# Three moves in a one-core kernel: sums of x over three periods, w_out2 decoded tile by tile earlier, one block's y copied by ScalarE

## The chip, the cores and the metric

The kernel runs on one core of a Trainium2 chip. The metric is the device time of one execution in microseconds (us). Before the change the median of three runs is 885.55 us (884.87 to 888.54).

## What is computed

Attention with a decaying state gives 3072 tokens of 512 values; two feed-forward layers follow. All in float32:

```python
for t in range(S):                      # 4 batches, 8 heads, S = 768, head size 64
    state = gamma * state + einsum('bhd,bhe->bhde', k[:, :, t], v[:, :, t])
    y[:, :, t] = scale * einsum('bhd,bhde->bhe', q[:, :, t], state)
x = y.transpose(0, 2, 1, 3).reshape(3072, 512)
h = x @ w_in                            # 512 x 2048
x = (h - tanh(h)) @ w_out               # 2048 x 512
h = x @ w_in2                           # 512 x 1024
sm = softmax(h)
solu = h * sm
ln = (solu - mean(solu)) / sqrt(var(solu) + 1e-6) * g_ln
out = ln @ w_out2                       # 1024 x 512
...
```

## The kernel before, in words

Each float32 operand of a product is split into a high and a low part (names ending in h and l), and a product is three matmuls: high by high, high by low, low by high. The weights come as 64-bit words and are decoded to float32 on the chip: a load "raw" on SP's queue (L124), an absolute value on ACT (L130), four integer and clamping operations on DVE (L137, L138, L141, L144), for w_out2 a scaling by g_ln on ACT (L152), the high part on ACT (L153) and the low part on DVE (L154). A Decoder object does one of these stages for one tile at a time with `to(stage, upto)`; its `step()` advances the whole line by one tile.

The tokens are worked in six blocks of 512. In order of time:

- 0 to 150 us: attention of the first blocks and the first layer's h of blocks 0 and 1.
- 150 to 238: the first pass, the product with w_out of blocks 0 and 1 (16 steps; the sums and parts of x for the next pair of blocks are made beside it, L580 to L583 and `put_x`). At its end `keep_y` copies four PSUM banks per block to SBUF, even ones by ACT (L388), odd ones by DVE (L386).
- 238 to 428: the second pass, h of blocks 2 to 5, two blocks at a time by a Strassen-like scheme of seven products P1 to P7 on halves of x and w_in, in 16 periods: eight for the pair (2, 3), eight for the pair (4, 5). It needs four sums of halves of x (`x_sums`) and a split of seven operands (`put_x`: high part xh on ACT, low part xl on DVE, L161). What remains of the attention runs between. A product's bank is added to a kept one by DVE (hs, L754) or subtracted from its tanh (L746, on POOL or DVE); only then does its bank come free for a product of a later period.
- 428 to 616: the product with w_out of blocks 2 to 5 (s = 2 to 5 in the code), 16 steps of 2.72 us each; operands g are loaded five steps ahead and split (gp) two steps ahead. The tiles of w_in2 and w_out2 are decoded here, and in the last block the first of six pairs of token groups goes through the second layer.
- 616 to 886: the second layer for the other pairs: product with w_in2 (L883), softmax and layer norm (L898 to L922), transposes (L933, with copies uh on ACT and ul on DVE, L936), product with w_out2 (L947).

In the first pass PE, ACT and part of POOL follow an order fixed in the program; from L700 on PE's order is the order of the code. For all other engines and for SP's queue a scheduler sets the order at build time, from its own estimate of times. Each engine then runs its list strictly in that order.

Of the kernel before, what the change touches and what calls it, by code (L numbers as in the profile page):

```python
# [26 lines left out]
F32 = mybir.dt.float32  # L27
F32R = mybir.dt.float32r
# [8 lines left out]
P = 128  # L37
# [53 lines left out]
def body(ctx: ExitStack, tc, z, w_in, w_out, w_in2, w_out2, g_ln, cst, tab, out):  # L91
# [2 lines left out]
    cpool = ctx.enter_context(tc.tile_pool(name="cpool", bufs=1))  # L94
    big = ctx.enter_context(tc.tile_pool(name="big", bufs=N4))
    mid = ctx.enter_context(tc.tile_pool(name="mid", bufs=N2))
    stp = ctx.enter_context(tc.tile_pool(name="stp", bufs=B + 2))
    yd = ctx.enter_context(tc.tile_pool(name="yd", bufs=1, space=DRAM))

    def pin(ins, on=True):  # L100
# [45 lines left out]
        ), fixed)  # L146

    def stage3(wf, scale, eng, fixed):
        w = t4([P, 2, 512], F32R, "w")
        hi, lo = w[:, 0, :], w[:, 1, :]  # L150
        if scale is not None:
            nc.scalar.activation(wf, wf, AF.Copy, scale=scale)  # L152
        pin(nc.scalar.copy(hi, wf), fixed)  # L153
        pin(eng.tensor_tensor(lo, wf, hi.bitcast(F32), ALU.subtract), fixed)  # L154
        return hi, lo
# [35 lines left out]
            self.to(2, i + 2)  # L191
            self.to(3, i + 1)

    A = ExitStack()
    G = ExitStack()
    xfp = A.enter_context(tc.tile_pool(name="xfp", bufs=1))
    ps_r = G.enter_context(tc.tile_pool(name="ps_r", bufs=4, space=PSUM))
# [181 lines left out]
                    py[e], a[:, cols], x, start=f == 0 and n == 0, stop=f == NF1 - 1 and n == 2  # L379
                )  # L380

    def keep_y(s, py):
        for e in range(NK):
            ysb = t2([P, SB], F32, "ysb")
            if e % 2:
                nc.vector.tensor_copy(ysb, py[e])  # L386
            else:
                nc.scalar.copy(ysb, py[e])  # L388
            nc.sync.dma_start(
                out=y1d[s][:, :, e, :], in_=ysb.rearrange("p (j t) -> p j t", j=B)  # L390
            )
# [66 lines left out]

    com = Combined()
    yl, ys, ysum = {}, {}, {}  # L460

    def load_y(j):
        t = t4([P, 2, NK, P], F32, "yl")
# [105 lines left out]
        wl[n] = views(t[:2], t[2:])  # L569

    def put_x(p, m, eng):
        xs[m] = [t4([P, 2, SB], F32R, f"x{n}") for n in "hl"]
        parts(*xs[m], sums[p][m], eng)

    def x_sums(p, other):

        x0, x1 = xf_of[2 * p], xf_of[2 * p + 1]
        b11, b21, b12, b22 = (x[:, h, :, :] for x in (x0, x1) for h in range(2))
        t1, t2_, t4_ = (t4([P, 2, SB], F32, "xt") for _ in range(3))
        nc.vector.tensor_tensor(t1, b12, b11, ALU.subtract)  # L580
        other.tensor_tensor(b12, b22, b12, ALU.subtract)
        nc.vector.tensor_tensor(t2_, b22, t1, ALU.subtract)
        other.tensor_tensor(t4_, b21, t2_, ALU.subtract)  # L583
        return {P1: b11, P2: b21, P3: b22, P5: t1, P6: t2_, P7: b12, P4: t4_}


    spare = dict(pool=ps_y, tag="y")
# [83 lines left out]
    for n in range(NF1 + 1):  # L671
        if n < NF1:
            while dec1.at[3] < NF1 + n + 1:
                dec1.step()
            if n:
                split_g(n)
            dec1.step()
        if n:
            for b, g in enumerate(gs.pop(n - 1)):
                products_y(n - 1, g, dec1.w[NF1 + n - 1], py2[b])  # L680
        if n in (9, 12, 15):
            load_wq()
        if n in (11, 14):
            combine_w(len(wl))
        if n in (13, 16):
            store_w()
        if n == 4:
            sums[1] = x_sums(1, nc.gpsimd)
        if 8 <= n < 15:
            put_x(1, n - 8, nc.vector)  # L690
        if n == 12:
            load_units(4 * B + 2)
        if n == 15:
            prepare(4 * B, H // 2, True, False)
    for b in range(2):
        keep_y(b, py2[b])
    G.close()


# [20 lines left out]
        else:  # L720
            unit(k, None, True, opool=ps_a)

    def product(left, m, ph, first=True):
        n = 0
        for i in range(2):
            (ah, al), (xh, xl) = ([t[:, i, :] for t in side[m]] for side in (left, xs))
            for a, x in ((ah, xh), (ah, xl), (al, xh)):
                nc.tensor.matmul(  # L728
                    ph, a, x, start=first and n == 0, stop=n == 5, skip_group_check=True
                )  # L730
                n += 1
# [54 lines left out]

    def begin(n):
        b1[n] = bank()
        product(wl[n], P1, b1[n])
        p1[n] = keep(b1[n])  # L790

    def after(n, m):
        if q[n] == (1, NJ1 - 1):
            put_x(2, m, nc.vector)

    begin(0)
    for n in range(len(q) + 1):
# [22 lines left out]
                split_wo(i)  # L820
        if now:
            b3 = bank()
            product(wl[n], P2, b3)
            finish(2 * p, j, summed(b3, p1.pop(n)), nc.gpsimd)
            piece(-1)
            after(n, P2)
            b2[n] = bank()
            product(wl[n], P5, b2[n])
            p5[n] = keep(b2[n])
            store_w()  # L830
            piece(0)
            after(n, P5)
            if todo:
                visit(todo.pop(0))
        if was:
            pp, jj = q[n - 1]
            product(wl[n - 1], P4, b1[n - 1], False)
            finish(2 * pp, jj + NJ1, b1.pop(n - 1), nc.vector)
            after(n - 1, P4)
        if now:  # L840
            product(wl[n], P6, b1[n], False)
            u2[n] = keep(b1[n])
            piece(1)
            after(n, P6)
            if todo:
                visit(todo.pop(0))
        if was:
            product(wl.pop(n - 1), P3, b2[n - 1], False)
            finish(2 * pp + 1, jj, summed(b2.pop(n - 1), u2.pop(n - 1)), nc.gpsimd)
            after(n - 1, P3)  # L850
        if now:
            if n + 1 < len(q):
                piece(2)
                begin(n + 1)
                after(n + 1, P1)
            product(wl[n], P7, b1[n], False)
            piece(3)
            finish(2 * p + 1, j + NJ1, summed(b1[n], p5.pop(n)), nc.gpsimd)
            after(n, P7)
            if todo:  # L860
                visit(todo.pop(0))
        if (p, j) == (1, 5):
            sums[2] = x_sums(2, nc.gpsimd)
    G.close()
    A.close()


    bp = ctx.enter_context(tc.tile_pool(name="bp", bufs=1))
    sp = ctx.enter_context(tc.tile_pool(name="sp", bufs=3))
    ident = bp.tile([P, P], F32, name="ident")  # L870
# [129 lines left out]
    for n, (s, f) in enumerate(steps):  # L1000
# [10 lines left out]
            keep_y(s, py)  # L1011
        if s >= NSB - 3 and n % 2 == 0 and com.n[2] < 12:
            com.step()
        if s == NSB - 1:
            if f % 2 and f > 4:
                dec2.step()
            if f == 0:
                load_y(0)
            if f == 2:
                sum_y(0)  # L1020
                load_y(1)
            if f == 5:
                split_y(0)
            if f == 9:
                sum_y(1)
                load_y(2)
            if f == 8:
                pair = Pair(0)
            for m in {8: (P1, P2), 9: (P6,), 10: (P5,), 11: (P7,), 12: (P4,), 13: (P3,)}.get(f, ()):
                pair.part(m)  # L1030
            if f == 12:
                split_y(1)
            if f == 14:
                sum_y(2)
# [10 lines left out]
    with tc.manual_schedule(engines={mybir.EngineType.PE}):  # L1045
        for j in range(1, NJ + 1):
# [8 lines left out]

            parts2(P1, P2)
            trans(a)
            dec2.step()
            parts2(P6, P5)
            trans(b)  # L1060
            dec2.step()
            if j + 2 < NJ:
                sum_y(j + 2)
            if j + 3 < NJ:
# [61 lines left out]
```

## Time and profile before

| | |
|---|---|
| time, median of 3 runs | 885.55 us (884.87 to 888.54) |
| profiled execution | 888.24 us, span 886.5 us |
| mean granted clock of TensorE in the span | 0.988 |
| PE busy | 842.8 us (95%), 6488 matmuls |
| DVE, ACT, POOL busy | 554.9, 437.3, 272.4 us (63%, 49%, 31%) |
| largest PE waits (table of waits) | 8.8 us for POOL vq (attention), 6.4 for DVE hs, 4.0 for DVE ul, 3.1 for ACT part, 2.9 for DVE gp, 2.4 for DVE ysb |

The profile is of one execution. Engines: PE is TensorE's matmuls, PEld its weight loads, DVE VectorE, ACT ScalarE, POOL GpSimd, SP the engine that issues most transfers. A row of a timeline gives the start and length in us, the engine, the line of the program, the operation, output <- inputs by the program's names, shapes and count; in brackets stands the time for which the engine was idle before it, and what ended that. Consecutive equal operations are drawn together (x4).

### The profile page before, as it was taken

The numbers are of one execution on the slowest core, as the hardware profiler recorded it, in microseconds if no ns is written. First come the engines' busy times: TensorE is split into PE (matmuls) and PEld (weight loads), VectorE is DVE, ScalarE is ACT, GpSimd is POOL, SyncE is SP. The second block draws the span as 40 slices with busy tenths as digits, with TensorE's granted clock in tenths as the row PEclk, the third lists the DMA queues.
The fourth block names the chain that finished last, engine by engine and source line by source line (L and its number), as shares of the span: only waits on it lengthen the run. The fifth ranks groups of instructions, "written<-read, shape, count | busy, mean of one in ns | idle before, by whom it ended". The sixth has DMA issues, their size and how long they took to land.

```text
span 886.5 us, 16612 instructions
## 1 busy us (share of the span) xinstructions
PE 842.8 (95%) x6488; PEld 693.1 (78%) x6488; DVE 554.9 (63%) x1025; ACT 437.3 (49%) x866; POOL 272.4 (31%) x244
## 2 busy tenths in 40 slices
PE   4799999999899988999999999989799999999997
PEld 4678888788777767888788888877688888888886
DVE  3798976999668686234546971397755555555541
ACT  4656644556445555445543451255555555555442
POOL 4410200212234354443201521045444444444200
PEclk8899999999999999999999999999999999999999
DMA  9667862535899518935857370743111111110001
GB/s 363 248 219 258 274 218 72 190 130 198 306 359 317 191 73 310 391 120 178 294 205 244 113 237 24 239 141 98 50 46 47 47 47 48 48 49 24 24 24 48
DMA packets 66462, 144.34 MB, mean 163 GB/s; under 512 B 6608, under 2 KB 19024, under 8 KB 66384
## 3 DMA queue, kind: packets, MB, share of 16 engines
q1 hardware_dynamic: 58032, 128.28, 41.2%
q10 hardware_dynamic: 8352, 15.00, 4.5%
q8 instruction: 51, 0.84, 0.4%
q14 instruction: 27, 0.22, 0.1%
HBM read 94.50 MB, written 48.76 MB: 162 GB/s over the span
## 4 chain that ended last, share of the span: by engine, by line
PE 77%; DVE 11%; DMA 5%; issue 3%; ACT 2%; SPq 1%; POOL 0%; ACTq 0%; POOLq 0%; DVEq 0%
PE py L378 20%; PE ph L728 15%; PE po L947 15%; PE ph L883 12%; PE ph L353 8%; PE out L229 2%; PE ptr L933 2%; PE sc L229 2%; DMA z<-z 2%; DVE wf L141 1%; DVE wcl L161 1%; DMA raw<-w_in 1%; DVE w L154 1%; DVE wf L138 1%; DMA wod<-wf 1%
## 5 line engine op out<-in xcount | busy, mean ns | idle before, releaser
L378 PE MATMUL py<-gp,w 128*128 128x512 f32 x768 | 176.0, 390 | 2.9 <-DVE gp L161 2.9
L378 PEld LDWEIGHTS py<-gp,w 128*128 128x128 f32 x768 | 143.9, 188 | 34.0 <-DVE gp L161 3.7
L947 PE MATMUL po<-w,uh 128*128 128x512 f32 x384 | 119.0, 391 | 0.0
L746 POOL TENSOR_TENSOR hs<-hs,th 128x512 f32<-128x512 f32 x48 | 65.7, 1371 | 101.2 <-ACT th L744 79.8
L947 PEld LDWEIGHTS po<-w,uh 128*128 128x128 f32 x384 | 72.4, 189 | 15.3
L353 PE MATMUL ph<-xh,w 128*128 128x512 f32 x256 | 82.1, 395 | 0.9 <-DVE w L154 0.9
L489 POOL TENSOR_TENSOR yla<-yl,yha 128x512 fp32r<-128x512 f32 (+1 forms) x24 | 35.6, 1504 | 151.0 <-PE po L947 85.6
L378 PE MATMUL py<-gh,w 128*128 128x512 f32 x256 | 79.3, 390 | 0.3 <-ACT gh L366 0.3
L947 PE MATMUL po<-w,ul 128*128 128x512 f32 x192 | 74.9, 390 | 0.0
L153 ACT CAST w<-wf 128x512 fp32r<-128x512 f32 x70 | 43.0, 620 | 61.7 <-DVE wf L144 53.5
L161 DVE TENSOR_TENSOR gp<-g,gp 128x512 fp32r<-128x512 f32 x64 | 51.6, 825 | 29.8 <-ACT gp L160 29.8
L728 PE MATMUL ph<-xh,wch 128*128 128x512 f32 x140 | 57.6, 411 | 8.0 <-DVE hs L754 5.6
L883 PE MATMUL ph<-w,yhs 128*128 128x512 f32 x192 | 62.1, 405 | 3.1 <-ACT part L890 3.1
L154 DVE TENSOR_TENSOR w<-wf,w 128x512 fp32r<-128x512 f32 x70 | 54.8, 787 | 11.2 <-ACT w L153 10.2
L744 ACT ACTIVATE th<-hs 128x512 f32<-128x512 f32 x48 | 30.3, 631 | 60.1 <-DVE hs L754 58.7
L353 PEld LDWEIGHTS ph<-xh,w 128*128 128x128 f32 x256 | 48.0, 188 | 12.0 <-DVE w L154 1.3
L378 PEld LDWEIGHTS py<-gh,w 128*128 128x128 f32 x256 | 48.0, 188 | 10.7 <-ACT gh L366 0.7
L754 DVE TENSOR_TENSOR hs<-ph,part 128x512 f32<-128x512 f32 x48 | 32.9, 687 | 36.5 <-PE ph L728 24.9
L728 PE MATMUL ph<-xh,wcl 128*128 128x512 f32 x140 | 55.2, 394 | 0.1
L728 PE MATMUL ph<-xl,wch 128*128 128x512 f32 x140 | 55.1, 394 | 0.0
L160 ACT CAST gp<-g 128x512 fp32r<-128x512 f32 x64 | 38.2, 617 | 34.1 <-DMA g<-gd 21.3
L728 PE MATMUL ph<-xh,wc 128*128 128x512 f32 x168 | 53.0, 391 | 1.4 <-DVE hs L754 0.8
(124 smaller groups left out, 1748.1 us busy)
## 6 DMA issues: line engine op xcount, KB each, us to landing
z<-z SPq DMA_DIRECT2D x48, 512.0 KB, 7.1
g<-gd SPq DMA_DIRECT2D x64, 256.0 KB, 5.3
raw<-w_in SPq DMA_DIRECT2D x24, 512.0 KB, 6.2
raw<-w_out SPq DMA_DIRECT2D x24, 512.0 KB, 4.3
gd<-hs SPq DMA_DIRECT2D x48, 256.0 KB, 2.9
y1d<-ysb SPq DMA_DIRECT2D x24, 256.0 KB, 3.3
wc<-wcd SPq DMA_DIRECT2D x12, 512.0 KB, 6.6
yl<-y1d SPq DMA_DIRECT2D x12, 512.0 KB, 4.1
```

The costliest lines, as they stand in the source:

```text
L153: pin(nc.scalar.copy(hi, wf), fixed)
L154: pin(eng.tensor_tensor(lo, wf, hi.bitcast(F32), ALU.subtract), fixed)
L160: nc.scalar.copy(h, src)
L161: eng.tensor_tensor(o, src, h.bitcast(F32), ALU.subtract)
L229: pin(nc.tensor.matmul(o, a, b, start=True, stop=True, skip_group_check=True), held[0])
L353: nc.tensor.matmul(ph, a[:, k, :], x, start=n == 0, stop=n == 3 * NK - 1), s < 2
L378: nc.tensor.matmul(py[e], a[:, cols], x, start=f == 0 and n == 0, stop=f == NF1 - 1 and n == 2)
L489: nc.gpsimd.tensor_tensor(o, src, h.bitcast(F32), ALU.subtract)
L728: nc.tensor.matmul(ph, a, x, start=first and n == 0, stop=n == 5, skip_group_check=True)
L746: eng.tensor_tensor(g, h, th, ALU.subtract)
L883: nc.tensor.matmul(ph, x[:, r, :], w, start=first and n == 0, stop=n == 5, skip_group_check=True)
L947: nc.tensor.matmul(po, a[:, f, :], b, start=f == 0 and n == 0, stop=f == NF2 - 1 and n == 2)
```

## The change

1. `x_sums` is cut in two. Step 0 makes one sum on DVE and one on POOL, step 1 the other two. In the first pass they stand at steps 4 and 6 (before: all at 4). For the second pair, step 0 stays at the end of period (1, 5), and step 1 and the seven splits are put at named products of the next two periods and the one after (`x_at`). All splits stood in period (1, 7) before.
2. The decoding of w_out2 (`dec2`) is called every third step from step 38 of the product with w_out (s = 4, f = 6), one stage of each of four tiles per call. Before it was called five times in the last block and three times in the loop over pairs. Its results go to a new pool of seven buffers; the room comes from a pool of the attention that now closes with the second pass.
3. `keep_y` of block 0 copies all four banks on ACT. Block 1 stays as it was.

```diff
@@ -94,7 +94,8 @@
     big = ctx.enter_context(tc.tile_pool(name="big", bufs=N4))
     mid = ctx.enter_context(tc.tile_pool(name="mid", bufs=N2))
-    stp = ctx.enter_context(tc.tile_pool(name="stp", bufs=B + 2))
+    A = ExitStack()
+    stp = A.enter_context(tc.tile_pool(name="stp", bufs=B + 2))
     yd = ctx.enter_context(tc.tile_pool(name="yd", bufs=1, space=DRAM))
@@ -146,7 +147,7 @@
 
     def stage3(wf, scale, eng, fixed):
-        w = t4([P, 2, 512], F32R, "w")
+        w = t4([P, 2, 512], F32R, "w") if scale is None or len(dec2.w) == NF2 - 1 else w2p.tile([P, 2, 512], F32R, name="w2")
         hi, lo = w[:, 0, :], w[:, 1, :]
@@ -191,7 +192,6 @@
             self.to(3, i + 1)
 
-    A = ExitStack()
     G = ExitStack()
@@ -379,10 +379,10 @@
                 )
 
-    def keep_y(s, py):
+    def keep_y(s, py, both=True):
         for e in range(NK):
             ysb = t2([P, SB], F32, "ysb")
-            if e % 2:
+            if e % 2 and both:
                 nc.vector.tensor_copy(ysb, py[e])
@@ -458,6 +458,11 @@
     com = Combined()
     yl, ys, ysum = {}, {}, {}
+
+    def step2(m):
+        for st, n in enumerate((m + 3, m + 2, m + 1, m)):
+            dec2.to(st, n)
+
 
@@ -569,19 +574,23 @@
 
     def put_x(p, m, eng):
-        xs[m] = [t4([P, 2, SB], F32R, f"x{n}") for n in "hl"]
-        parts(*xs[m], sums[p][m], eng)
-
-    def x_sums(p, other):
+        xs[p, m] = [t4([P, 2, SB], F32R, f"x{n}") for n in "hl"]
+        parts(*xs[p, m], sums[p][m], eng)
+
+    def x_sums(p, step):
 
         x0, x1 = xf_of[2 * p], xf_of[2 * p + 1]
         b11, b21, b12, b22 = (x[:, h, :, :] for x in (x0, x1) for h in range(2))
-        t1, t2_, t4_ = (t4([P, 2, SB], F32, "xt") for _ in range(3))
-        nc.vector.tensor_tensor(t1, b12, b11, ALU.subtract)
-        other.tensor_tensor(b12, b22, b12, ALU.subtract)
-        nc.vector.tensor_tensor(t2_, b22, t1, ALU.subtract)
-        other.tensor_tensor(t4_, b21, t2_, ALU.subtract)
-        return {P1: b11, P2: b21, P3: b22, P5: t1, P6: t2_, P7: b12, P4: t4_}
+        if step == 0:
+            t1 = t4([P, 2, SB], F32, "xt")
+            nc.vector.tensor_tensor(t1, b12, b11, ALU.subtract)
+            nc.gpsimd.tensor_tensor(b12, b22, b12, ALU.subtract)
+            sums[p] = {P1: b11, P2: b21, P3: b22, P5: t1, P7: b12}
+        else:
+            t2_, t4_ = (t4([P, 2, SB], F32, "xt") for _ in range(2))
+            nc.vector.tensor_tensor(t2_, b22, sums[p][P5], ALU.subtract)
+            nc.gpsimd.tensor_tensor(t4_, b21, t2_, ALU.subtract)
+            sums[p] |= {P6: t2_, P4: t4_}
 
@@ -685,7 +694,9 @@
             store_w()
         if n == 4:
-            sums[1] = x_sums(1, nc.gpsimd)
+            x_sums(1, 0)
+        if n == 6:
+            x_sums(1, 1)
         if 8 <= n < 15:
@@ -693,7 +704,7 @@
             prepare(4 * B, H // 2, True, False)
     for b in range(2):
-        keep_y(b, py2[b])
+        keep_y(b, py2[b], b > 0)
     G.close()
...
@@ -786,12 +797,19 @@
     def begin(n):
         b1[n] = bank()
-        product(wl[n], P1, b1[n])
+        product(wl[n], q[n][0], P1, b1[n])
         p1[n] = keep(b1[n])
 
+    x_at = {
+        (NJ1 - 1, P2): P1, (NJ1 - 1, P5): P2, (NJ1 - 1, P6): P5, (NJ1 - 1, P7): P6,
+        (NJ1, P2): P7, (NJ1, P6): P4, (NJ1, P7): P3,
+    }
+
     def after(n, m):
-        if q[n] == (1, NJ1 - 1):
-            put_x(2, m, nc.vector)
+        if n == NJ1 - 2 and m == P5:
+            x_sums(2, 1)
+        if (n, m) in x_at:
+            put_x(2, x_at[n, m], nc.vector)
 
...
@@ -853,18 +871,19 @@
                 begin(n + 1)
                 after(n + 1, P1)
-            product(wl[n], P7, b1[n], False)
+            product(wl[n], p, P7, b1[n], False)
             piece(3)
             finish(2 * p + 1, j + NJ1, summed(b1[n], p5.pop(n)), nc.gpsimd)
             after(n, P7)
             if todo:
                 visit(todo.pop(0))
         if (p, j) == (1, 5):
-            sums[2] = x_sums(2, nc.gpsimd)
+            x_sums(2, 0)
     G.close()
     A.close()
 
 
+    w2p = ctx.enter_context(tc.tile_pool(name="w2p", bufs=7))
     bp = ctx.enter_context(tc.tile_pool(name="bp", bufs=1))
@@ -1011,9 +1030,10 @@
         if s >= NSB - 3 and n % 2 == 0 and com.n[2] < 12:
             com.step()
+        m = n - 2 * NF1 - 6
+        if m >= 0 and m % 3 == 0:
+            step2(m // 3)
         if s == NSB - 1:
-            if f % 2 and f > 4:
-                dec2.step()
             if f == 0:
@@ -1055,10 +1075,8 @@
             parts2(P1, P2)
             trans(a)
-            dec2.step()
             parts2(P6, P5)
             trans(b)
-            dec2.step()
             if j + 2 < NJ:
```

Rows of the engines' lists follow, of the program before and of the changed one, with a row's number and line; the changed program's lines are 1 to 19 higher (L161 is L162 there, on ACT L160 is L161; L526 to L529 are L531 to L534; L738, L746, L754 are L749, L757, L765; L898, L910, L936 are L917, L929, L955).

ACT at the handover from the first pass to the second, before. wch are high parts of w_in, vq the scalings that wait for a z transfer, ysb the copies of `keep_y`; P1 of the second pass needs the bank of the first copy.

```order
212 L160 CAST wch<-wq 128x512
213 L160 CAST wch<-wq 128x256
214 L388 COPY ysb<-py 128x512
215 L248 ACTIVATE vq<-z,con 128x64 x4
216 L388 COPY ysb<-py 128x512 x3
217 L248 ACTIVATE vq<-z,con 128x64 x4
218 L738 COPY part<-ph 128x512
```

The same place of the changed program:

```order
210 L161 CAST wch<-wq 128x512
211 L161 CAST wch<-wq 128x256
212 L248 ACTIVATE vq<-z,con 128x64 x4
213 L388 COPY ysb<-py 128x512 x6
214 L248 ACTIVATE vq<-z,con 128x64 x4
215 L749 COPY part<-ph 128x512
216 L755 ACTIVATE th<-hs 128x512
217 L749 COPY part<-ph 128x512
```

All copies now stand behind the four scalings; there were one ahead of them and three behind.

DVE in the last two periods of the pair (2, 3), before: from the sum that is made right after the hs that ends PE's first wait to the two hs of which the first ends PE's second wait. xl are low parts of x, wcl those of w_in and its sums.

```order
423 L529 TENSOR_TENSOR wsum<-wq,wsum 128x256
424 L161 TENSOR_TENSOR wcl<-wsum,wch 128x512
425 L754 TENSOR_TENSOR hs<-ph,part 128x512
426 L161 TENSOR_TENSOR xl<-xf,xh 128x1024
427 L161 TENSOR_TENSOR wcl<-wsum,wch 128x512
428 L161 TENSOR_TENSOR xl<-xf,xh 128x1024
429 L161 TENSOR_TENSOR xl<-xt,xh 128x1024
430 L746 TENSOR_TENSOR th<-ph,th 128x512
431 L754 TENSOR_TENSOR hs<-ph,part 128x512
432 L161 TENSOR_TENSOR xl<-xt,xh 128x1024
433 L161 TENSOR_TENSOR xl<-xf,xh 128x1024
434 L754 TENSOR_TENSOR hs<-ph,part 128x512 x2
```

The same stretch of the changed program, from L534 just ahead of the hs of the first wait to the hs of the second:

```order
419 L534 TENSOR_TENSOR wsum<-wq,wsum 128x256
420 L765 TENSOR_TENSOR hs<-ph,part 128x512
421 L162 TENSOR_TENSOR wcl<-wsum,wch 128x512
422 L765 TENSOR_TENSOR hs<-ph,part 128x512
423 L162 TENSOR_TENSOR xl<-xf,xh 128x1024
424 L162 TENSOR_TENSOR wcl<-wsum,wch 128x512
425 L162 TENSOR_TENSOR xl<-xf,xh 128x1024
426 L757 TENSOR_TENSOR th<-ph,th 128x512
427 L765 TENSOR_TENSOR hs<-ph,part 128x512
428 L162 TENSOR_TENSOR xl<-xt,xh 128x1024 x2
429 L765 TENSOR_TENSOR hs<-ph,part 128x512 x2
```

One xl fewer stands between the two, and L534 has moved ahead of the first.

DVE at the first pair behind the last block, before. L137 to L154 are the decode, hn and ul the operations for which ACT and PE wait.

```order
614 L386 COPY ysb<-py 128x512
615 L137 TENSOR_SCALAR wf<-wf 128x512
616 L912 TENSOR_SCALAR hn<-ex,us 128x1024
617 L137 TENSOR_SCALAR wf<-wf 128x512
618 L138 TENSOR_SCALAR wf<-wf 128x512 x2
619 L141 SCALAR_TENSOR_TENSOR wf<-raw,wf 128x512 x2
620 L918 TENSOR_SCALAR ssq<-ssq,ssum 128x1
621 L144 SCALAR_TENSOR_TENSOR wf<-raw,wf 128x512 x2
622 L919 TENSOR_SCALAR ssq<-ssq 128x1
623 L898 ISA hn,nm<-ph_6920,part 128x512
624 L898 ISA nm 128x1
625 L936 TENSOR_TENSOR ul<-ptr,uh 128x512 x2
```

The same stretch of the changed program:

```order
625 L155 TENSOR_TENSOR w<-wf,w 128x512
626 L386 COPY ysb<-py 128x512
627 L930 TENSOR_SCALAR us<-us 128x1
628 L936 RECIPROCAL ssum<-ssum 128x1
629 L386 COPY ysb<-py 128x512
630 L931 TENSOR_SCALAR hn<-ex,us 128x1024
631 L937 TENSOR_SCALAR ssq<-ssq,ssum 128x1
632 L938 TENSOR_SCALAR ssq<-ssq 128x1
633 L917 ISA hn,nm<-ph_6936,part 128x512
634 L917 ISA nm 128x1
635 L955 TENSOR_TENSOR ul<-ptr,uh 128x512 x4
636 L917 ISA hn,nm<-ph_6968,part 128x512
```

The decode has gone from between L912 (L931) and ul; one low part (L155) is left ahead.

## Rows read from the trace of the kernel before

**Rows 1.** Windows: stretch, length, busy (x instructions) PE PEld DVE ACT POOL, PEclk, DMA, GB/s

```profile
340.00:360.00 20.00, 20.00 (x83) 16.39 (x83) 9.04 (x11) 9.39 (x17) 10.24 (x7) 0.93 1.02 385
520.00:540.00 20.00, 20.00 (x90) 16.53 (x90) 11.98 (x19) 10.77 (x20) 0.00 (x0) 1.00 0.60 207
540.00:560.00 20.00, 20.00 (x90) 16.57 (x89) 2.77 (x4) 2.16 (x4) 2.86 (x4) 1.00 0.13 41
600.00:620.00 20.00, 18.38 (x82) 14.60 (x81) 14.46 (x27) 11.64 (x21) 11.87 (x9) 1.00 0.32 102
620.00:640.00 20.00, 15.39 (x67) 12.14 (x66) 15.24 (x27) 10.55 (x19) 8.07 (x10) 0.91 0.19 57
```

**Rows 2.** Timeline of PE around 242: start, length, engine, operation [idle before <-releaser]

```profile
241.85 0.50 PE L728 MATMUL ph<-xh,wch 128*128 128x512 f32 x1 [2.40 <-DVE ysb L386]
```

**Rows 3.** Timeline of ACT, same stretch

```profile
236.82 0.58 ACT L388 COPY ysb<-py 128x512 f32<-128x512 f32 x1
238.97 1.07 ACT L248 ACTIVATE vq<-z,con 128x64 f32<-128x64 f32 x4 [1.56 <-DMA z<-z]
```

**Rows 4.** Timeline of DVE, same stretch

```profile
239.32 2.47 DVE L386 COPY ysb<-py 128x512 f32<-128x512 f32 x4
```

**Rows 5.** Timeline of PE, 326 to 340

```profile
326.93 0.50 PE L728 MATMUL ph<-xh,wch 128*128 128x512 f32 x1 [2.79 <-DVE hs L754]
...
339.69 0.79 PE L728 MATMUL ph<-xh,wch 128*128 128x512 f32 x1 [2.79 <-DVE hs L754]
```

**Rows 6.** Timeline of DVE, 320 to 339

```profile
321.28 2.30 DVE L526 TENSOR_TENSOR wsum<-wq 128x256 f32<-128x256 f32 x1
...
325.53 0.41 DVE L527 TENSOR_TENSOR wsum<-wsum,wq 128x256 f32<-128x256 f32 x1
...
335.62 1.21 DVE L161 TENSOR_TENSOR xl<-xt,xh 128x1024 fp32r<-128x1024 f32 x1
336.75 2.29 DVE L161 TENSOR_TENSOR xl<-xf,xh 128x1024 fp32r<-128x1024 f32 x1
```

**Rows 7.** Timeline of POOL, 320 to 339

```profile
320.90 2.40 POOL L583 TENSOR_TENSOR xt<-xf,xt 128x1024 f32<-128x1024 f32 x1 [1.22 <-DVE xt L582]
...
336.50 1.46 POOL L746 TENSOR_TENSOR hs<-hs,th 128x512 f32<-128x512 f32 x1 [4.83 <-issue]
```

**Rows 8.** Timeline of PE, 581 to 630

```profile
581.97 2.81 PE L378 MATMUL py<-gp,w 128*128 128x512 f32 x11 [1.24 <-DVE gp L161]
...
591.49 0.73 PE L883 MATMUL ph<-w,yhs 128*128 128x512 f32 x2 [1.28 <-ACT part L890]
...
614.05 2.81 PE L378 MATMUL py<-gp,w 128*128 128x512 f32 x11 [1.62 <-DVE gp L161]
...
622.48 0.72 PE L883 MATMUL ph<-w,yhs 128*128 128x512 f32 x2 [1.79 <-ACT part L890]
...
628.32 1.25 PE L933 MATMUL ptr<-ident,hn 128*128 128x128 f32 x8 [2.81 <-DVE ul L936]
```

**Rows 9.** Timeline of ACT, 590 to 591

```profile
590.24 0.72 ACT L152 ACTIVATE wf<-wf,gl 128x512 f32<-128x512 f32 x1 [7.52 <-DVE wf L144]
```

**Rows 10.** Timeline of DVE, 596 to 628

```profile
597.45 0.42 DVE L137 TENSOR_SCALAR wf<-wf 128x512 f32<-128x512 f32 x1
597.90 0.43 DVE L138 TENSOR_SCALAR wf<-wf 128x512 int32<-128x512 int32 x1
598.36 0.69 DVE L141 SCALAR_TENSOR_TENSOR wf<-raw,wf 128x512 int32<-128x512 int32 x1
599.09 0.69 DVE L144 SCALAR_TENSOR_TENSOR wf<-raw,wf 128x512 int32<-128x512 int32 x1
...
623.62 3.37 DVE L144 SCALAR_TENSOR_TENSOR wf<-raw,wf 128x512 int32<-128x512 int32 x2
...
627.58 1.28 DVE L936 TENSOR_TENSOR ul<-ptr,uh 128x512 fp32r<-128x512 f32 x2
```

**Rows 11.** Page, DMA issues: operation xcount, KB each, median us to landing

```profile
raw<-w_out SPq DMA_DIRECT2D x24, 512.0 KB, 4.3
```

More of the change, by code (lines that the diff above doesn't have):

```diff
@@ L721, in visit, with product @@
             unit(k, None, True, opool=ps_a)
-    def product(left, m, ph, first=True):
+    def product(left, p, m, ph, first=True):
         n = 0
         for i in range(2):
-            (ah, al), (xh, xl) = ([t[:, i, :] for t in side[m]] for side in (left, xs))
+            (ah, al), (xh, xl) = ([t[:, i, :] for t in side] for side in (left[m], xs[p, m]))
             for a, x in ((ah, xh), (ah, xl), (al, xh)):
@@ L822, in body @@
             b3 = bank()
-            product(wl[n], P2, b3)
+            product(wl[n], p, P2, b3)
             finish(2 * p, j, summed(b3, p1.pop(n)), nc.gpsimd)
@@ L827, in body @@
             b2[n] = bank()
-            product(wl[n], P5, b2[n])
+            product(wl[n], p, P5, b2[n])
             p5[n] = keep(b2[n])
@@ L836, in body @@
             pp, jj = q[n - 1]
-            product(wl[n - 1], P4, b1[n - 1], False)
+            product(wl[n - 1], pp, P4, b1[n - 1], False)
             finish(2 * pp, jj + NJ1, b1.pop(n - 1), nc.vector)
@@ L840, in body @@
         if now:
-            product(wl[n], P6, b1[n], False)
+            product(wl[n], p, P6, b1[n], False)
             u2[n] = keep(b1[n])
@@ L847, in body @@
         if was:
-            product(wl.pop(n - 1), P3, b2[n - 1], False)
+            product(wl.pop(n - 1), pp, P3, b2[n - 1], False)
             finish(2 * pp + 1, jj, summed(b2.pop(n - 1), u2.pop(n - 1)), nc.gpsimd)
```

## The prediction

> **What bounds the kernel now.** I read the page first: PE is busy for 95% of the span, the other engines for far less, so only time in which PE stands still, or runs at its lower clock, can be won. The table of waits then names whom PE waits for (DVE's hs, ul, gp and ysb, ACT's part), and PE's timeline says where. Three places touch the change.
>
> - The handover from the first pass to the second: at 241.85 the first matmul of P2 has stood 2.40 us for a copy ysb of DVE [rows 2]. DVE makes four of them in a row, 2.47 us from 239.32 [rows 4]; PE goes on when they are done.
> - The x of the third pair of blocks, 315 to 344: two stalls of 2.79 us, at 326.93 and 339.69, both for an hs of DVE [rows 5], whose queue has no gap there. After the second the windows show a granted clock of 0.93 for 340 to 360 [rows 1].
> - The last block of the second product and the first pair after it: stalls of 1.24, 1.28, 1.62, 1.79 and 2.81 us, 8.74 together [rows 8], and a granted clock of 0.91 in 620 to 640 [rows 1]. Decode operations of w_out2 stand ahead on the queue of the engine that PE waits for: at 590.24 ACT scales a tile, having waited 7.52 us for DVE, and the copy "part" comes behind it [rows 9]; at 623.62 DVE's two L144 take 3.37 us, and ul follows at 627.58 [rows 10].
>
> Elsewhere from 245 to 860 PE runs with few gaps, none of them at code that moves.
>
> **The change part by part.** No arithmetic is added or taken away; places change, and the engine of two copies. Sums are made against the profiled execution, 888.24 us (span 886.5, 1.7 around it). It lies 2.69 us above the median of the runs shown, 885.55; I subtract the gain from the median unchanged.
>
> *First block's y on ACT.* DVE loses two of its four copies, 1.2 us (2.47 / 4 each [rows 4]); ACT gets two. ACT's order changes with it: before, the copy for which P1 of the second pass waits ran at 236.82, ahead of four scalings that stood for a z transfer until 238.97 [rows 3]; now these scalings come first and all six copies behind them. P1 can then start at about 238.97 + 1.07 + 0.58 = 240.6 [rows 3], 2.7 later than its 237.9 (P2's 241.85 less the stall of 2.40 and P1's own 1.5). P1 done at 242.1, P2 goes straight on, since DVE's last copy is now ready at 239.3 + 1.2 + 0.1 = 240.6. Where P2 starts at 241.85 today, it starts at about 242: the wait has gone over from P2 to P1. Term 0. Bounds: 2.40 won if z lands early enough, 2 lost if z lands some 2 us later, since P1 now hangs on it.
>
> *Sums and parts of x over three periods.* DVE's and POOL's sums run against each other: a wsum takes 0.41 at 325.53, and its like took 2.30 at 321.28, beside POOL's sum of 2.40 from 320.90 [rows 6, 7]. Up to the hs of the first stall the new order has the same operations of DVE and POOL with one more wsum (0.41); only which of them stand beside POOL's two sums changes. Term 0, bounds from 1.9 lost (2.30 - 0.41, one more caught) to 2.79 won.
>
> The Trainium skill, "SBUF — State Buffer", section "Who interferes with whom", says that a DVE instruction with two inputs in SBUF and a GpSimd instruction that reads SBUF need one port, and that the later of them stands until the other is done. The 2.30 against 0.41 agrees. By this rule a sum put a period later takes its stop along, to whatever of DVE comes next, and the term is 0; if a short operation could pass beside POOL's, the wsum now behind the first sum would go by in 0.8 us, and 1.9 us more would be won, 872.8 in all.
>
> Between the two stalls DVE has five xl before, the last 2.29 long beside POOL where one takes 1.21 [rows 6, 7], and four now; the fifth comes behind the hs that PE awaits. POOL's four subtractions there are the same. So that hs comes 1.2 earlier and the second stall shrinks from 2.79 to 1.6. A stall of 1.62 at 614.05 [rows 8] left the clock of 600 to 620 at 1.00 [rows 1], so I take the slow stretch of 340 to 360 as gone, (1 - 0.93) x 20 = 1.4 [rows 1]. Term 1.2 + 1.4 = 2.6; bounds 0 (POOL stops one operation more) and 2.79 + 1.4 = 4.2. The xl that are pushed back fall into 340 to 360, where DVE is busy for 9.04 of 20 us [rows 1]; without that gap each costs 1.2.
>
> *w_out2 tile by tile from block 4 on.* A tile costs DVE 0.42 + 0.43 + 0.69 + 0.69 us [rows 10] and a subtraction that I set at another 0.69: 2.9 us. Four tiles are decoded in the second half of block 4, four in block 5 before the pair's first hn, all but one subtraction. The cover in block 4: from 520 to 540 DVE is busy for 11.98, from 540 to 560 for 2.77 of 20 us, POOL for 0 and 2.86 [rows 1]; 4 x 2.9 = 11.6 us go into gaps of 8.0 and 17.2. From the pair's first part on no decode stands before part, ul or hn any longer: the stalls at 591.49, 622.48 and 628.32 go, 1.28 + 1.79 + 2.81 = 5.9 [rows 8], and the slow clock, (1 - 0.91) x 20 = 1.8 [rows 1]. The stall at 614.05 is a gp behind the pair's own softmax operations and beside POOL; that stays, 1.62. The one at 581.97 is a gp behind decode, and three tiles are still decoded near it: I count half of 1.24, 0.6. Term 5.9 + 1.8 + 0.6 = 8.3; bounds 0 (stalls that only move) and 8.74 + 1.8 = 10.5. The new loads stand on SP ahead of g loads and wait there for PE to free a buffer; g is loaded five steps ahead of its use, of which a wait of one or two costs nothing.
>
> The sums of the first pass at two steps, and the pool that is freed earlier, lie where PE has no wait: 0.
>
> Sum: 0 + 2.6 + 8.3 = 10.9; 885.55 - 10.9 = 874.6 us.
>
> **The rivals.**
> 1. *All three places come clear.* z lands in time and both x stalls go: 885.55 - (2.40 + 2.79 + 4.2 + 8.3) = 867.9. For it: DVE has less to do ahead of each wait. Against: z came at 238.97 and POOL's sums are as long as before.
> 2. *The x stalls stay.* POOL's subtractions catch one more operation of DVE ahead of the awaited hs, 2.29 - 1.21 = 1.1, which eats the xl saved: 885.55 - 8.3 = 877.2. For it: DVE's queue there has the same operations in all, without a gap.
> 3. *The decode gives its gain back.* gp stands behind decode in blocks 4 and 5 as at 581.97: seven tiles x 1.24 = 8.7 eats the 8.3. Left is x: 885.55 - 2.6 = 883.0. Against: POOL hardly runs from 520 to 560 [rows 1].
> 4. *Slower: DVE waits for raw words.* DVE runs in order. If it reaches a tile's L142 (L141 before) ahead of the raw load's landing, every gp behind it is late. A load takes 4.3 us [rows 11] and gp is made two steps ahead, so that is free as long as SP issues the load early. It decides from 10.9 / 8 = 1.4 us of PE standing per tile; at the 2.81 of the longest stall in [rows 8] it is 22.5, and the time 874.6 + 22.5 = 897.1. Against: on SP the loads stand several steps ahead of their decode.
>
> **How the numbers follow.** Forecast 0.58, rival 1 0.07, rival 2 0.20, rival 3 0.09, rival 4 0.06. A measurement of this kernel tells about 0.5%, 4.4 us, from no change; faster is below 881.1. The forecast's own spread, with the handover and the halves of the two terms, is some 870 to 880, and 0.02 of its chance lies above 881.1. Faster: 0.56 + 0.07 + 0.20 = 0.83. Same: rival 3 and that tail, 0.11. Slower: 0.06. The range of 868 to 882 has rivals 1 and 2 within or at its edge and leaves out rival 4, most of rival 3 and some tails.
>
> **What would show it.** Right: P1 of the second pass starts near 240.6, with P2 right behind; the hs stall near 337 is about 1.6 us and the clock after it 1.00; DVE is busier by some 10 us in 520 to 560; no wait for part or ul in the last block and the first pair, clock 1.00 there, one gp stall of about 1.6 left. Wrong: a P1 that waits over 4 us (z, not the copies, sets the handover), an hs stall of 2.8 or more, gp stalls in block 4, DVE waiting for raw.

## The result, and the profile after

The changed kernel takes 873.82 us (median of 4 runs, 871.51 to 875.72) against 886.49 for the kernel before on the same chip: ratio 0.9855, 95% interval 0.9821 to 0.9888. A second measurement gave 875.99 against 888.22, 0.9875 (0.9846 to 0.9905). The forecast was 874.6, with a range of 868 to 882. The profiled execution took 874.34, its span 872.6 at a mean clock of 0.992.

PE's timeline at the three places, to be read against [rows 2, 5, 8]:

```profile
238.72 0.50 PE L739 MATMUL ph<-xh,wch 128*128 128x512 f32 x1 [0.34 <-ACT ysb L388]
...
240.21 0.40 PE L739 MATMUL ph<-xh,wch 128*128 128x512 f32 x1
...
324.27 0.50 PE L739 MATMUL ph<-xh,wch 128*128 128x512 f32 x1 [2.63 <-DVE hs L765]
...
336.74 0.50 PE L739 MATMUL ph<-xh,wch 128*128 128x512 f32 x1 [2.03 <-DVE hs L765]
...
419.95 0.50 PE L739 MATMUL ph<-xh,wc 128*128 128x512 f32 x1 [0.78 <-DVE hs L765]
...
605.99 2.79 PE L378 MATMUL py<-gp,w 128*128 128x512 f32 x11 [1.55 <-DVE gp L162]
...
613.38 0.73 PE L902 MATMUL ph<-w,yhs 128*128 128x512 f32 x2 [1.01 <-ACT part L909]
...
616.25 1.04 PE L952 MATMUL ptr<-ident,hn 128*128 128x128 f32 x8
```

P2 of the second pass (240.21) waits for nothing; P1 stood 0.34 us. Both hs stalls are still there. Of the five stalls of [rows 8] two are left, 1.55 and 1.01; the transposes, which stood 2.81 us for ul, start at once (616.25).

The same windows as in [rows 1], and the one from 320 to 340, of the changed kernel:

```profile
320.00:340.00 20.00, 15.01 (x64) 11.48 (x63) 20.00 (x18) 13.85 (x21) 11.69 (x7) 1.00 0.44 152
340.00:360.00 20.00, 20.00 (x90) 16.54 (x90) 8.84 (x11) 9.34 (x17) 9.48 (x7) 1.00 0.93 343
520.00:540.00 20.00, 20.00 (x90) 16.57 (x89) 19.09 (x35) 14.92 (x26) 0.00 (x0) 1.00 0.77 284
540.00:560.00 20.00, 20.00 (x90) 16.57 (x89) 7.06 (x10) 4.72 (x8) 3.57 (x4) 1.00 0.37 114
600.00:620.00 20.00, 17.44 (x84) 14.08 (x83) 15.96 (x30) 12.27 (x22) 18.99 (x18) 1.00 0.28 80
620.00:640.00 20.00, 20.00 (x98) 16.75 (x97) 10.09 (x27) 10.96 (x19) 9.92 (x11) 1.00 0.16 53
```

DVE (third number pair) carries 11.4 us more from 520 to 560, with PE full; PE is full from 620 to 640, and the clock is 1.00 in all these windows.

The first 240 us of one and the same kernel differ by some us between executions: P2 starts at 240.21 in one profile of the changed kernel and at 243.44 in another (number 9). So I compare lengths between the starts of fixed points of PE's program: the last matmul of the first pass ("last y"), P2, the matmul behind the second pass's last hs wait (424.81 before, 419.95 after), and the end of the span. All are in us.

| stretch | before | after | after, second profile |
|---|---|---|---|
| last y of the first pass to P2 | 4.15 | 2.22 | 1.59 |
| P2 to the last hs wait | 182.96 | 179.74 | 180.70 |
| last hs wait to the end of the span | 461.6 | 452.6 | 452.6 |

That is a gain of about 2 (to 2.6) at the handover, 3.2 or 2.3 in the second pass, 9.0 behind it. The column before is one execution. Number 7 leaves all code behind the first pass as it was before, and its profile took 459.3 us from the last hs wait to the end: against that one the gain there is 6.7. The stalls for part and ul are the same in both (1.79 and 2.81 us behind the last block), but the granted clock of 620 to 640, 0.91 before [rows 1], is 1.00 in number 7:

```profile
620.00:640.00 20.00, 17.19 (x80) 13.88 (x79) 16.13 (x32) 12.30 (x22) 10.77 (x10) 1.00 0.12 41
```

### The profile page after: what moved, and what is told of

The parts are those of the page before. It is cut to its first block, busy times and chain, and to the rows that moved or that the text cites. A ratio compares the mean times of both kernels' runs of the same rounds, so it can differ in the third digit from the quotient of the medians.

```text
span 872.6 us, 16582 instructions
## 1 busy us (share of the span) xinstructions
PE 838.4 (96%) x6488; PEld 691.3 (79%) x6488; DVE 551.0 (63%) x1023; ACT 438.6 (50%) x868; POOL 286.6 (33%) x244
## 4 chain that ended last, share of the span: by engine, by line
PE 81%; DVE 8%; DMA 4%; ACT 3%; issue 2%; SPq 1%; POOL 0%; ACTq 0%; POOLq 0%; DVEq 0%
PE py L378 25%; PE po L966 15%; PE ph L739 14%; PE ph L902 13%; PE ph L353 8%; PE out L229 2%; PE ptr L952 2%; DMA z<-z 2%; PE sc L229 2%; DMA raw<-w_in 1%; DVE wcl L162 1%; DMA wod<-wf 1%; DVE wsum L532 1%; DVE hs L765 0%; DVE wf L145 0%
## 5 line engine op out<-in xcount | busy, mean ns | idle before, releaser
L757 POOL TENSOR_TENSOR hs<-hs,th 128x512 f32<-128x512 f32 x48 | 66.5, 1391 | 94.3 <-ACT th L755 81.2
L154 ACT CAST w<-wf 128x512 fp32r<-128x512 f32 x70 | 43.0, 620 | 56.8 <-DVE wf L145 48.8
L162 DVE TENSOR_TENSOR gp<-g,gp 128x512 fp32r<-128x512 f32 x64 | 49.7, 788 | 18.8 <-ACT gp L161 18.6
L155 DVE TENSOR_TENSOR w<-wf,w 128x512 fp32r<-128x512 f32 x70 | 50.5, 726 | 11.2 <-ACT w L154 10.2
L765 DVE TENSOR_TENSOR hs<-ph,part 128x512 f32<-128x512 f32 x48 | 32.8, 686 | 34.6 <-PE ph L739 20.4
L927 ACT ACTIVATE ex<-hn,nm 128x1024 f32<-128x1024 f32 x24 | 27.7, 1153 | 53.1 <-DVE nm L917 52.1
```

Source lines behind the costliest of these rows:

```text
L162: eng.tensor_tensor(o, src, h.bitcast(F32), ALU.subtract)
L757: eng.tensor_tensor(g, h, th, ALU.subtract)
L765: nc.vector.tensor_tensor(h, ph, part, ALU.add)
```

## The experiments

Times are medians in us; ratios are to the kernel before on the same chip, with the 95% interval. Lengths between fixed points come from the one profile of each run.

**1. The copies put back.**

```diff
-        keep_y(b, py2[b], b > 0)
+        keep_y(b, py2[b])
```

> The changed kernel with only the copies put back: block 0's y is again copied half by DVE, half by ACT. Measured in the changed kernel: P2 of the second pass starts at 240.21 where it started at 241.85, though P1 was held until 238.72. Theory A (the gain at the handover comes from z and w_in landing 1.8 us earlier, the copies give nothing): P1 again starts near 238.7 behind the scalings, P2 near 240.2, DVE's fourth copy is done by 239.8, and the time stays at 873.8 within 1 us. Theory B (the copies on ACT free P2): P2 waits for DVE's fourth copy, starts near 241.8, and the time is 875.5 to 876.

Measured: 877.39, 0.9898 (0.9878 to 0.9918); last y to P2 2.32 us. The length of the handover stayed, as theory A has it; but P1 waited for nothing (238.05), and it was P2 that stood 0.47 us for DVE's copy. The time is 3.6 above the changed kernel's first measurement and 1.4 above its second; the intervals overlap. In the profile the difference lies in the second pass: 182.5 us from P2 to the last hs wait, where the changed kernel took 179.74. There the granted clock fell behind the second hs stall, as it did in the kernel before (0.91 in this window too), and not in the changed kernel's first profile:

```profile
330.00:350.00 20.00, 17.66 (x70) 13.77 (x69) 16.39 (x15) 11.72 (x18) 10.47 (x7) 0.91 0.78 255
```

No run ties that to the copies.

**2. The first pass's sums put back to one step.**

```diff
             x_sums(1, 0)
-        if n == 6:
             x_sums(1, 1)
```

> The changed kernel with only the first pass's sums back at one step (both at step 4 instead of steps 4 and 6). Theory A (that split lets DVE and SP run ahead, so that z lands earlier): the z that ACT's scalings wait for lands near 239 again instead of 237.1, P2 of the second pass starts near 241.8, time 875.5 to 876. Theory B (the split in the first pass does nothing, the copies do it): z lands near 237, P2 at 240.2, time 873.8 within 1 us.

Measured: 875.73, 0.9882 (0.9862 to 0.9902), which can't be told from the changed kernel; last y to P2 3.23 us. PE waits again for DVE's ysb:

```profile
242.43 0.50 PE L738 MATMUL ph<-xh,wch 128*128 128x512 f32 x1 [1.49 <-DVE ysb L386]
```

SP's queue (start, length of the issue, operation) in the kernel before and in the changed one shows why:

```profile
230.01 0.46 SPq L512 DMA_DIRECT2D wq<-wfd  x1
230.52 2.73 SPq L212 DMA_DIRECT2D z<-z  x4
```

```profile
229.15 0.42 SPq L517 DMA_DIRECT2D wq<-wfd  x1
229.62 2.35 SPq L212 DMA_DIRECT2D z<-z  x4
```

Counted back from the last y, this load of w_in (wq, with z behind it) is issued 7.7 us ahead before (237.70 - 230.01) and 8.8 after. In all profiles with one step it is 7.7 to 7.8, in all with two 8.8 to 8.9. It stands on SP right behind a store of a low part of w_in that DVE makes. With two steps SP reaches the loads 1.1 us earlier, so theory A.

**3. The second pair's sums and splits put back.** `x_sums(2, 0)` and `x_sums(2, 1)` both at the end of period (1, 5), all seven splits in period (1, 7):

```diff
-    x_at = { ...
+    x_at = {(NJ1 - 1, m): m for m in range(7)}
```

> The changed kernel with only the second pair's sums and splits back where they were: all four sums at the end of period (1, 5), all seven splits in period (1, 7). My theory (one split less stands ahead of the awaited hs, and the clock stays up): stalls of about 2.7 and 2.8 us near 324 and 337, granted clock near 0.93 in the 20 us behind them, time up by 2 to 2.5 us, 876. Rival (the place of the splits does not matter, DVE's queue is full either way): stalls as in the changed kernel (2.6 and 2.0), clock 1.00, 873.8 within 1 us.

Measured: 874.23, 0.9871 (0.9839 to 0.9903): no slower than the changed kernel. PE in its profile:

```profile
326.97 0.79 PE L739 MATMUL ph<-xh,wch 128*128 128x512 f32 x1 [2.81 <-DVE hs L765]
...
339.75 0.50 PE L739 MATMUL ph<-xh,wch 128*128 128x512 f32 x1 [1.48 <-DVE hs L765]
```

The windows of the same profile:

```profile
320.00:340.00 20.00, 15.72 (x62) 12.24 (x61) 20.00 (x21) 11.75 (x18) 8.13 (x5) 0.91 0.30 96
```

The second stall is short here because the clock fell behind the first: PE worked more slowly and came later to the second hs, which DVE ends. So stall lengths do not compare. What the move changes is the length from the first awaited hs to the second: 12.76 to 12.79 us with the old places (three profiles), 12.46 to 12.49 with the new (six), and the first stall, 2.79 to 2.81 against 2.63 to 2.64. My expectation of the time fell; the rival holds but for these 0.5 us.

**4. The decode put back, the new pool kept.**

```diff
-        m = n - 2 * NF1 - 6
-        if m >= 0 and m % 3 == 0:
-            step2(m // 3)
         if s == NSB - 1:
+            if f % 2 and f > 4:
+                dec2.step()
...
             trans(a)
+            dec2.step()
             parts2(P6, P5)
             trans(b)
+            dec2.step()
```

> The changed kernel with only the decoding of w_out2 back in the last block and the loop over pairs. My theory (this part carries 9 us of the 12.7 to 13.9): PE waits for gp, part and ul again, 8 to 9 us of stalls from 570 to 625 and a granted clock near 0.91 in the last 20 us of that stretch, time 882 to 884. Rival (part of these stalls came from the softmax operations and POOL and only moved with the decode): time 877 to 880.

Measured: 877.75, 0.9900 (0.9874 to 0.9925); last hs wait to end 454.1. Time and stalls both miss my theory: two stalls stand there, of which only the one for ul came back (2.02); the one for gp is in the changed kernel too (1.55).

```profile
607.12 2.79 PE L378 MATMUL py<-gp,w 128*128 128x512 f32 x11 [1.56 <-DVE gp L162]
...
618.26 1.25 PE L952 MATMUL ptr<-ident,hn 128*128 128x128 f32 x8 [2.02 <-DVE ul L955]
```

The time is the rival's, but not for its reason, as the next two show.

**5. The pool alone**, in the kernel before: the seven buffers of w_out2's tiles, decode where it was.

```diff
-        w = t4([P, 2, 512], F32R, "w")
+        w = t4([P, 2, 512], F32R, "w") if scale is None or len(dec2.w) == NF2 - 1 else w2p.tile([P, 2, 512], F32R, name="w2")
```

> The kernel before with only the new pool: seven tiles of w_out2 get buffers of their own, the decode is called where it was. With the decode put back but the pool kept, the time was 877.75, not the 882 to 884 I expected, and the last two raw loads were issued at 589 instead of 604. Theory P (the decode was late because its tiles and raw words waited for buffers of the shared pool; own buffers cure most of it): the last raw loads go out near 590 to 600, stalls for part and ul shrink by 4 to 6 us in all, time 880 to 882. Theory W (where the decode is called decides): stalls of 581 to 630 as before, time 886.5 within 1 us.

Measured: 880.73, 0.9925 (0.9898 to 0.9952); last hs wait to end 454.0, 7.6 less than before and 5.3 less than number 7. Two of the five stalls are left:

```profile
607.83 2.80 PE L378 MATMUL py<-gp,w 128*128 128x512 f32 x11 [1.56 <-DVE gp L162]
...
618.98 1.25 PE L934 MATMUL ptr<-ident,hn 128*128 128x128 f32 x8 [2.02 <-DVE ul L937]
```

The last loads of w_out2 on SP, before and with the pool alone:

```profile
584.80 0.33 SPq L124 DMA_DIRECT2D raw<-w_out  x1
...
604.07 4.41 SPq L124 DMA_DIRECT2D raw<-w_out  x2
```

```profile
577.22 0.33 SPq L125 DMA_DIRECT2D raw<-w_out  x1
...
589.75 4.41 SPq L125 DMA_DIRECT2D raw<-w_out  x2
```

The last two tiles are asked for 14 us earlier, 11 when both are counted from the last hs wait (424.81 and 421.50), with not one call moved. Before, raw words and decoded tiles shared forty buffers with the other tiles of that size, and the loads stood for one: from 500 to 640 SP's raw loads waited 9.1 us for DVE's gp and 23.7 for PE, with the pool alone 1.6 and 21.7.

**6. The new places, the shared pool.**

```diff
-        w = t4(...) if scale is None or len(dec2.w) == NF2 - 1 else w2p.tile(...)
+        w = t4([P, 2, 512], F32R, "w")
```

> The changed kernel with w_out2's tiles in the shared pool again, decode called at the new places. Theory P (the buffers decide): raw and yl loads wait for the shared buffers, some of the stalls between 570 and 630 come back, time 876 to 880. Theory W (the places decide): as the changed kernel, 873.8 within 1 us.

Measured: 876.30, 0.9873 (0.9851 to 0.9895); last hs wait to end 454.3, 7.3 less than before, 1.7 more than with both. A gp stall is back at 576, and those for gp and part stay:

```profile
576.17 2.79 PE L378 MATMUL py<-gp,w 128*128 128x512 f32 x11 [1.35 <-DVE gp L162]
...
606.64 2.79 PE L378 MATMUL py<-gp,w 128*128 128x512 f32 x11 [1.61 <-DVE gp L162]
...
614.02 0.73 PE L901 MATMUL ph<-w,yhs 128*128 128x512 f32 x2 [1.00 <-ACT part L908]
```

So either edit alone takes away most of what both do: 7.3 to 7.6 of 9.0 against the profile before, 5.0 to 5.3 of 6.7 against number 7. Each does it in its own way: the places take the decode off the queue ahead of ul; with the pool alone the decode still runs through the last block, but its last integer step on DVE (L145, L144 before) comes 5 to 6 us earlier (195.5 us behind the last hs wait, against 201.5 before and 200.7 in number 7). Neither theory was right alone.

**7. The copies alone**, in the kernel before, with the edit of number 1 turned round.

> The kernel before with only block 0's copies on ACT. In this build two copies stand ahead of the four scalings on ACT, so P1 does not hang on z. Theory A (what came early at the handover is z and w_in; DVE's queue still holds the copies up until its low parts of w_in are done at 239.4): z lands near 239, P2 starts at 240.6 with two copies instead of four, a gain of 1.2, time 885.3. Theory B (the copies alone bring the 1.9 us): P2 at 240.0 or before, time 884.5. Rival (nothing): 886.5.

Measured: 886.84 against 887.62, 0.9991 (0.9971 to 1.0011): no change that can be told. Last y to P2 is 2.93 us, 1.2 less than before, as theory A has it; 1.2 us is what this measurement can't see.

**8. All sums of the second pair on DVE.**

```diff
-            nc.gpsimd.tensor_tensor(b12, b22, b12, ALU.subtract)
+            (nc.vector if p > 1 else nc.gpsimd).tensor_tensor(b12, b22, b12, ALU.subtract)
...
-            nc.gpsimd.tensor_tensor(t4_, b21, t2_, ALU.subtract)
+            (nc.vector if p > 1 else nc.gpsimd).tensor_tensor(t4_, b21, t2_, ALU.subtract)
```

> The changed kernel with all four sums of the second pair on DVE, none on POOL. In the changed kernel L533 and L532 took 2.61 and 2.59 beside POOL's sums where one takes 0.41. Theory port (DVE stands while POOL runs a sum): both fall to about 0.4, 4.4 us less, against two more sums of 1.2 on DVE, 2.3 more; the stall near 324 falls from 2.6 to about 0.5, time about 871.5 to 872. Rival (DVE is simply full there; two sums more make it longer): the stall near 324 grows to 4 to 5, time 875.5 to 876.

Measured: 871.02, 0.9816 (0.9793 to 0.9839). DVE and POOL in the changed kernel:

```profile
314.88 2.61 DVE L533 TENSOR_TENSOR wsum<-wq 128x256 f32<-128x256 f32 x1
...
320.09 2.59 DVE L532 TENSOR_TENSOR wsum<-wsum,wq 128x256 f32<-128x256 f32 x1
```

```profile
314.77 2.44 POOL L587 TENSOR_TENSOR xf<-xf 128x1024 f32<-128x1024 f32 x1 [2.48 <-DVE xt L586]
319.97 2.42 POOL L592 TENSOR_TENSOR xt<-xf,xt 128x1024 f32<-128x1024 f32 x1 [2.76 <-DVE xt L591]
```

DVE, and then PE, without POOL's sums:

```profile
313.56 0.42 DVE L533 TENSOR_TENSOR wsum<-wq 128x256 f32<-128x256 f32 x1
...
317.70 0.41 DVE L532 TENSOR_TENSOR wsum<-wsum,wq 128x256 f32<-128x256 f32 x1
```

```profile
320.84 0.50 PE L739 MATMUL ph<-xh,wch 128*128 128x512 f32 x1 [0.53 <-DVE hs L765]
...
332.38 0.50 PE L739 MATMUL ph<-xh,wch 128*128 128x512 f32 x1 [1.72 <-DVE hs L765]
```

Two more sums on DVE, and its queue is shorter by 2.1 us up to the first hs: the stall falls from 2.63 to 0.53. That is the port theory in its operations and its stall; the time lies 0.5 below its range. The interval overlaps that of the changed kernel's first measurement, not that of the second; from P2 to the last hs wait the profile took 177.0 us, where the seven with the new places and POOL's sums took 179.7 or more.

**9. The changed kernel again**, as reference for the next two.

> The changed kernel once more, on the chip of the next two, as their reference: 873.8 within 1.5 us, and between the last y of the first pass and P2 about 2.0 us (3.9 before).

Measured: 875.99, 0.9875 (0.9846 to 0.9905), 0.7 above my bound. Its profile has the same first hs stall as the first one, but a low clock behind it:

```profile
328.03 0.79 PE L739 MATMUL ph<-xh,wch 128*128 128x512 f32 x1 [2.64 <-DVE hs L765]
```

```profile
320.00:340.00 20.00, 17.36 (x64) 13.71 (x63) 20.00 (x19) 10.66 (x16) 10.11 (x6) 0.83 0.30 101
```

PE then works so slowly that it never waits for the second hs. The stall's length alone does not decide it: 2.63 was followed by 1.00, 2.64 by 0.83.

**10. Both edits of the first pass put back**, those of numbers 1 and 2.

> The changed kernel with both edits of the first pass undone: its sums at one step and the copies half on DVE. From the last y of the first pass to P2 the runs so far show 3.9 us with neither edit, 2.7 with the copies alone, 3.0 with the split alone undone, 2.1 with the copies alone undone, 2.0 with both edits. Theory A (the two edits of the first pass give 1.9 us there, mostly by z and w_in being asked for 1.1 us earlier): 3.9 us there again, time 1.5 to 2.5 above the changed kernel. Rival (what is won at the handover is lost at the next wait): 3.9 us there, and the time within 0.8 of the changed kernel.

Measured: 876.57, 0.9893 (0.9857 to 0.9929), 0.6 above number 9 with intervals that overlap widely; last y to P2 3.40 us. The handover is longer, as both theories have it, by 1.2 to 1.8 us against the profiles with both edits; the time fits the rival. (The lengths in the expectations of numbers 9 and 10 are counted from some 0.2 us after the start of the last y.) Between the two the measurement cannot decide.

**11. All sums on DVE, and the next pair's split called at step 9 of the last block, not 12.**

```diff
                 load_y(2)
+                split_y(1)
...
-            if f == 12:
-                split_y(1)
```

> The kernel with all second-pair sums on DVE (871.0, against 887.6 for the kernel before), and the split of the second pair of token groups called three steps earlier in the last block (step 9, not 12), where POOL is idle from 580 to 600. Theory port (the gp behind the 1.55 us stall stood 2.9 us beside POOL's yls): that gp takes 0.7, the stall goes, the wait for part (1.0) shrinks, time 868.5 to 869.5. Rival (the gp waits for the softmax operations ahead of it on DVE): the stall stays above 1 us, time 870.5 to 871.5.

Measured: 867.70, 0.9786 (0.9757 to 0.9815), 8.3 us below the changed kernel on the same chip: the fastest version, 0.8 below the port theory's range. The two edits are together here; the earlier split's own part shows behind the last hs wait, 449.5 us to the end against 452.7 in number 8. In the changed kernel the gp for the last step took 2.90 us beside POOL's yls (DVE and POOL):

```profile
603.04 2.90 DVE L162 TENSOR_TENSOR gp<-g,gp 128x512 fp32r<-128x512 f32 x1
```

```profile
603.01 2.38 POOL L494 TENSOR_TENSOR yls<-ysum,yhs 128x1024 fp32r<-128x1024 f32 x1
```

With the earlier split, DVE, and the window behind it:

```profile
596.61 0.68 DVE L162 TENSOR_TENSOR gp<-g,gp 128x512 fp32r<-128x512 f32 x1
```

```profile
600.00:620.00 20.00, 20.00 (x98) 16.72 (x97) 12.93 (x29) 12.23 (x24) 9.83 (x12) 1.00 0.28 80
```

PE has no gap left there: the waits for gp and for part are gone.

## Why the prediction was right or wrong

**The total was right, its parts less so, and that is in part luck.** Forecast 0 + 2.6 + 8.3 = 10.9; measured 12.7, or 12.2 the second time. A handover that I had too low by 2 stood against an x term that I had too high by about as much, and some 2 of the 9.0 us of the decode are not there against a second profile of the old code (number 7, below).

**Handover, term 0: too low by about 2.** That P1 would hang on z and P2 follow at once came true in the first profile, not in number 9, the same kernel, where P1 waits for nothing. ACT in the first profile, columns as in [rows 3]:

```profile
237.13 1.06 ACT L248 ACTIVATE vq<-z,con 128x64 f32<-128x64 f32 x4 [2.26 <-DMA z<-z]
238.10 2.99 ACT L388 COPY ysb<-py 128x512 f32<-128x512 f32 x6
```

But z came at 237.13, not 238.97. The step that failed is the one on the rest, "The sums of the first pass at two steps ... lie where PE has no wait: 0". PE waits for nothing there, but SP's loads do, and they get a head start of 1.1 us (number 2). Numbers 1, 2, 7 and 10 show both edits at work: 3.4 to 4.2 us from y to P2 with neither, 2.9 and 3.2 with the copies alone, 2.3 with the split of the sums alone, 1.6 to 2.2 with both; so the split does more than the copies. In the whole time these 2 us could not be told from nothing (numbers 7 and 10).

**Sums and parts of x, term 2.6: too high, the mechanism wrong.** "That hs comes 1.2 earlier": it came 0.3 earlier (12.76 to 12.47 us from first to second hs). The failed step is "POOL's four subtractions there are the same". Before, three of them fall between the two awaited hs, and three operations of DVE are long: these two and the xl of 336.75 [rows 6].

```profile
328.33 2.20 DVE L161 TENSOR_TENSOR xl<-xf,xh 128x1024 fp32r<-128x1024 f32 x1
...
330.45 1.78 DVE L161 TENSOR_TENSOR wcl<-wsum,wch 128x512 fp32r<-128x512 f32 x1
```

In the changed order the hs of three products come within 3.2 us (322.60 to 325.78), POOL's subtractions follow in a bunch, four of them fall between the awaited hs, and beside them four operations of DVE are longer by about 1.1 us each (changed kernel, DVE and POOL):

```profile
324.14 1.72 DVE L162 TENSOR_TENSOR wcl<-wsum,wch 128x512 fp32r<-128x512 f32 x1
...
327.51 1.78 DVE L162 TENSOR_TENSOR wcl<-wsum,wch 128x512 fp32r<-128x512 f32 x1
...
329.22 2.30 DVE L162 TENSOR_TENSOR xl<-xf,xh 128x1024 fp32r<-128x1024 f32 x1
...
332.64 3.44 DVE L162 TENSOR_TENSOR xl<-xt,xh 128x1024 fp32r<-128x1024 f32 x2
```

```profile
324.02 1.29 POOL L757 TENSOR_TENSOR hs<-hs,th 128x512 f32<-128x512 f32 x1 [1.62 <-ACT th L755]
326.49 3.94 POOL L757 TENSOR_TENSOR hs<-hs,th 128x512 f32<-128x512 f32 x2 [1.18 <-ACT th L755]
...
333.52 1.48 POOL L757 TENSOR_TENSOR hs<-hs,th 128x512 f32<-128x512 f32 x1 [3.08 <-issue]
```

One more of about 1.1 us, so rival 2 in miniature. The second stall shrank by 0.76 (2.79 to 2.03): 0.3 of that is the earlier hs, the rest is PE coming later to it, 0.34 us of it for ACT's part at 330.33, and no gain.

The 1.4 us of clock can't be put down to the change. The low stretch comes behind the first stall, behind the second or not at all: behind the second in the kernel before and in number 1, behind the first in numbers 2, 3, 5, 6, 7 and 9, nowhere in the changed kernel's first profile and in numbers 4 and 10. So all four profiles with the old places have it and four of the seven with the new; one kernel had it in one execution and not in another (number 9). From P2 to the last hs wait the profiles with the old places took 180.9 to 183.3 us (four), those with the new ones and POOL's sums 179.7 to 182.5 (seven), 1.5 less in the mean; the stalls as such make 0.5 of it, and the rest is within the spread of either group. The two profiles whose clock fell behind the second stall, where PE can't make it up in a later wait for hs, differ by no more than that: 182.96 before, 182.54 in number 1.

For the first stall I weighed whether a short operation could pass beside POOL's sum, and said no. L533 stood 2.61 us beside POOL's sum, 0.42 without it. The Trainium skill's rule in "SBUF — State Buffer", section "Who interferes with whom", agrees. Number 8 shows the price: without POOL's two sums the ratio is 0.9816, where the changed kernel's two measurements are 0.9855 and 0.9875, 0.4 to 0.6% of 887 or 3.5 to 5.2 us, with intervals that overlap in the first case.

**Decode of w_out2, term 8.3: near in size, half right in cause.** Of the stalls for part and ul those of 1.28 and 2.81 went, and of the 1.79 for part 1.01 stayed, against the forecast; the gp stall that I put down to the softmax and POOL stayed as forecast (1.55, forecast 1.62), and number 11 shows that POOL makes it; DVE filled 520 to 560 by 11.4 us (forecast some 10). Measured against the profile before, the term is 9.0, against number 7's it is 6.7: the clock of 620 to 640, which I took for a part of the stalls' price, fell in the one and not in the other behind the same 1.79 and 2.81 us. I credited the places. The seven own buffers got no term (I put only "the pool that is freed earlier", which makes room for them, at 0), and they do as much alone (7.6 us against the profile before, 5.3 against number 7's) as the places alone (7.3 and 5.0), as numbers 5 and 6 show. Rivals 3 and 4 did not come: no gp stall stands in block 4.

## What to carry to other kernels

A wait is read from its queue, but what filled the queue late can be a buffer: ask of each tile moved which pool it leaves and which loads stood for that pool. An edit where PE never waits is not free of effect while a transfer's issue hangs on it. Where one engine's operation stands while another's runs, as DVE's beside POOL's here, giving both sums to one of them can be faster than sharing. A stretch of low clock in one profile is no term of a sum until a second profile of the same code shows it.

## What the runs showed of the hardware that was not expected

A 128x256 subtraction of DVE took 2.6 us beside a 2.4 us sum of POOL, 0.41 alone; two sums more on DVE made DVE's queue shorter. The granted clock behind stalls of the same length (2.63 and 2.64) was 1.00 in one execution and 0.83 over 20 us in another of the same kernel; behind 1.79 and 2.81 us it was 0.91 before and 1.00 in number 7. Up to the end of the first pass two executions of one kernel differed by 3.9 us (its last y at 237.99 and 241.85).
